# A 1 KB vector in a full DMA stream: one piece behind the start-up barriers, or sixteen pieces ahead of them

## The chip, the cores and the metric

The kernel runs on 1 core of one Trainium2 chip. The time is device microseconds of that core. A run of one core has no second die to compare with, so its state is called fast where it lies with the fastest runs of the same kernel; all runs here are fast but one, which is marked (a single run, state unknown). "The span" is the time from the first to the last instruction in the profile; it is 1.2 to 1.4 us shorter than the time of the same run.

## The reference

```python
B, S, D = 1024, 16, 512          # x, y: bf16 [1024, 16, 512]; gamma: bf16 [512]
def reference(x, y, gamma):
    return x + gamma * y
```

x and y are 16.78 MB each, and so is the result. Gamma is 1 KB.

## The kernel before

Each of the 128 partitions holds 128 rows of 512 elements. SP (SyncE) issues the loads of y and x, ACT (ScalarE) issues gamma and the two stores. `EARLY` says how many transfers of each of the two are put ahead of the program's start-up barriers, at which all engines wait for each other before the program proper begins (in the profile of before SP sits 0.2 us at the first of them and 0.5 us at the two that follow): one of SP (y's first half), none of ACT.

```python
SP = [('y', 0, 64), ('x', 0, 64, 0), ('y', 64, 128), ('x', 64, 117, 0), ('x', 117, 128, 64)]
ACT = [('g',), ('s', 0, 64), ('s', 64, 128)]
EARLY = (1, 0)
DVE = [('m', 0), ('m', 1), ('a', 0), ('a', 1), ('m', 2), ('m', 3), ('a', 2), ('a', 3)]
# ... (cut)
gamma_row = nc.alloc_sbuf_tensor("gamma_row", [1, D], dt).ap()
# ... (cut: in the loop that issues the transfers)
if kind == "g":
    i = eng.dma_start(out=gamma_row, in_=gamma.unsqueeze(0)).then_inc(s_gamma, 16)
# ... (cut)
# a row of ones times gamma's row: TensorE copies gamma to all 128 partitions
nc.tensor.matmul(gamma_ps, ones_row, gamma_row, start=True, stop=True).then_inc(s_ps, 1)
nc.vector.tensor_copy(out=gamma_sb, in_=gamma_ps).then_inc(s_dve, 1)
```

VectorE then multiplies y by gamma ("m") and adds x ("a"), in pieces of 53 and 11 rows. x's rows from 64 on go to the place of the first ones, so their load waits for the first add.

## Time and profile before

| | before |
|---|---|
| time, median of 6 runs | 120.09 us (119.85 to 120.28) |
| span in the profile | 118.6 us |
| the 16 DMA engines, two queues | 66.0% + 32.6% of the span |
| VectorE busy | 70.0 us, 59% |
| gamma: issue, landing, first use | 1.43, 9.60, 21.94 us |

The table of waits names who sat idle (engine, tile and line, what ended it: us in total, times, longest):

```profile
DVE y_sb L156 <- DVEq L25: 12.7, 2, 10.8
...
DVE y_sb L165 <- DVEq L25: 2.2, 1, 2.2
```

Line 156 is the multiply, line 165 the add, and line 25 is the helper that waits on a semaphore. VectorE waits 10.8 us for y ahead of the first multiply, and another 2.2 us for x ahead of the first add. The timeline (start, us, instruction) shows what that add releases:

```profile
41.39 17.29 DVE L165 TENSOR_TENSOR y_sb<-x_sb,y_sb 128x27136 bf16<-128x27136 bf16 x2 [2.16 <-DVEq L25]
55.71 0.81 SPq L113 DMA_DIRECT2D x_sb<-in_x_dram  x2
```

x's later loads are issued as soon as the first add is over; y's second half keeps the DMA engines busy until about 60 us (its last landing is at 60.49 us).

### The profile page before, as it was taken

The page shows a single profiled execution, that of the slowest core. Times are in us where ns is not written, and L with a number is a line of the kernel's source. Part 1 is how long each engine was busy: PE and PEld are TensorE (multiplying, and loading weights), DVE is VectorE, ACT ScalarE, POOL GpSimd, SP SyncE. Part 2 cuts the span into 40 slices and gives each one's busy share as a digit, 9 for nine tenths or more (in the row PEclk, how much of TensorE's full clock was granted, in tenths as well). Part 3 has the DMA queues.
Part 4 walks back from the last instruction along what each step waited for, and adds up shares of the span by engine and source line. Part 5 has one row for each costly group of instructions (what it writes and reads, how often), then busy time and mean ns, then how long its engine had stood idle before and what let it go on. Part 6 is the DMA issues. An engine that isn't in the chain of part 4 may idle for free. (4 is left out here: it accounts for less than half of the span.)

```text
span 118.6 us, 78 instructions
## 1 busy us (share of the span) xinstructions
PE 0.6 (0%) x1; PEld 0.1 (0%) x1; DVE 70.0 (59%) x10; POOL 0.2 (0%) x4
## 2 busy tenths in 40 slices
PE   0001000000000000000000000000000000000000
PEld 0000000000000000000000000000000000000000
DVE  0002000599999299999759999999999910000000
POOL 0000000000000000000000000000000000000000
DMA  9889888998899888998896969598899888988892
GB/s 354 354 376 685 354 354 354 597 464 354 354 398 663 354 354 354 663 398 354 354 586 293 586 293 567 220 639 354 354 575 486 354 354 376 685 354 354 354 619 88
DMA packets 1010, 50.33 MB, mean 424 GB/s; under 512 B 113, under 2 KB 114, under 8 KB 114
## 3 DMA queue, kind: packets, MB, share of 16 engines
q1 hardware_dynamic: 720, 33.55, 66.0%
q10 hardware_dynamic: 290, 16.78, 32.6%
HBM read 33.56 MB, written 16.78 MB: 424 GB/s over the span
## 5 line engine op out<-in xcount | busy, mean ns | idle before, releaser
L156 DVE TENSOR_TENSOR y_sb<-y_sb,gamma_sb 128x27136 bf16<-128x27136 bf16 (+1 forms) x4 | 34.6, 8688 | 12.7 <-DVEq L25 12.7
L165 DVE TENSOR_TENSOR y_sb<-x_sb,y_sb 128x27136 bf16<-128x27136 bf16 (+1 forms) x4 | 34.6, 8688 | 2.3 <-DVEq L25 2.2
L132 DVE CAST gamma_sb<-gamma_ps 128x512 bf16<-128x512 f32 x1 | 0.7, 692 | 8.8 <-DVEq L25 8.8
L127 DVE MEMSET ones_row<- 1x128 bf16 x1 | 0.2, 165 | 1.5 <-PEq L41 1.5
L130 PE MATMUL gamma_ps<-gamma_row,ones_row 1*128 1x512 bf16 x1 | 0.6, 578 | 9.7 <-PEq L25 9.7
L130 PEld LDWEIGHTS gamma_ps<-gamma_row,ones_row 1*128 1x128 bf16 x1 | 0.1, 100 | 9.7 <-issue 9.7
L194 POOL MEMSET const-uint8-127<- 128x1 uint8 x1 | 0.1, 102 | 0.0
L194 POOL MEMSET const-bfloat16-1.0<- 128x1 bf16 x1 | 0.1, 101 | 0.0
L194 POOL MEMSET const-float32-0.0<- 128x1 f32 x1 | 0.1, 98 | 0.2 <-issue 0.2
L194 POOL MEMSET const-float32-1.0<- 128x1 f32 x1 | 0.1, 98 | 0.0
## 6 DMA issues: line engine op xcount, KB each, us to landing
x_sb<-in_x_dram SPq DMA_DIRECT2D x1, 6784.0 KB, 20.8
x_sb<-in_x_dram SPq DMA_DIRECT2D x1, 1408.0 KB, 23.9
y_sb<-in_y_dram SPq DMA_DIRECT2D x2, 40.2
out_dram<-y_sb ACTq DMA_DIRECT2D x2, 22.8
x_sb<-in_x_dram SPq DMA_DIRECT2D x1, 39.7
gamma_row<-in_gamma_dram ACTq DMA_DIRECT2D x1, 1.0 KB
```

What stands on the lines that cost most here:

```text
L127: nc.vector.memset(ones_row, 1.0).then_inc(s_ones, 1)
L130: nc.tensor.matmul(gamma_ps, ones_row, gamma_row, start=True, stop=True).then_inc(s_ps, 1)
L132: nc.vector.tensor_copy(out=gamma_sb, in_=gamma_ps).then_inc(s_dve, 1)
L156: nc.vector.tensor_tensor(out=yt, in0=yt, in1=g, op=MULT).then_inc(s_dve, 1)
L165: nc.vector.tensor_tensor(out=yt, in0=xt, in1=yt, op=ADD).then_inc(s_add, 1)
L194: nc = _bacc.Bacc("TRN2", target_bir_lowering=False, num_devices=1)
```

## The change

Its intent: gamma is asked for at the very start and shared evenly among the engines, so that it arrives early and no one engine carries it alone. It becomes sixteen pieces of 64 B, meant as one for each DMA engine, which lie 128 B apart in one partition, and TensorE reads them as one row.

```diff
-EARLY = (1, 0)
+EARLY = (1, 1)
...
-    gamma_row = nc.alloc_sbuf_tensor("gamma_row", [1, D], dt).ap()
+    gamma_row = nc.alloc_sbuf_tensor("gamma_row", [1, 16, D // 8], dt).ap()[:, :, : D // 16]
...
-                i = eng.dma_start(out=gamma_row, in_=gamma.unsqueeze(0)).then_inc(s_gamma, 16)
+                src = gamma.rearrange("(a k d) -> a k d", a=1, k=16)
+                i = eng.dma_start(out=gamma_row, in_=src).then_inc(s_gamma, 16)
...
-    nc.tensor.matmul(gamma_ps, ones_row, gamma_row, start=True, stop=True).then_inc(s_ps, 1)
+    nc.tensor.matmul(gamma_ps.rearrange("p (k d) -> p k d", k=16), ones_row, gamma_row, start=True, stop=True).then_inc(s_ps, 1)
```

## The prediction

> **What bounds the kernel now.** I read the page first, from the busy times down to the DMA queues, to see which resource is full.
>
> ```profile
> PE 0.6 (0%) x1; PEld 0.1 (0%) x1; DVE 70.0 (59%) x10; POOL 0.2 (0%) x4
> ...
> DMA  9889888998899888998896969598899888988892
> ...
> DMA packets 1010, 50.33 MB, mean 424 GB/s; under 512 B 113, under 2 KB 114, under 8 KB 114
> ## 3 DMA queue, kind: packets, MB, share of 16 engines
> q1 hardware_dynamic: 720, 33.55, 66.0%
> q10 hardware_dynamic: 290, 16.78, 32.6%
> ```
>
> The two queue shares add up to 98.6% of sixteen engines over the whole span of 118.6 us. VectorE, the only compute engine with real work, is busy 59%. So the DMA engines are full, and bytes (x and y in, the sum out, 50.33 MB) set the time. The packet counts will matter too: seven large transfers (two of y, three of x, two stores) leave one 4 byte semaphore write per engine, 7 x 16 = 112, and 113 packets are under 512 B. The 113th is the single semaphore write of gamma, and the step from 113 to 114 is gamma itself, one packet of 1024 B.
>
> Then the timeline of the first 23 us and the table of waits, to see where gamma stands:
>
> ```profile
> 0.00 0.37 SPq L116 DMA_DIRECT2D y_sb<-in_y_dram  x1
> ...
> 1.43 0.33 SPq L113 DMA_DIRECT2D x_sb<-in_x_dram  x1
> 1.43 0.52 ACTq L110 DMA_DIRECT2D gamma_row<-in_gamma_dram  x1
> ...
> 9.73 0.58 PE L130 MATMUL gamma_ps<-gamma_row,ones_row 1*128 1x512 bf16 x1 [9.73 <-PEq L25]
> 10.46 0.69 DVE L132 CAST gamma_sb<-gamma_ps 128x512 bf16<-128x512 f32 x1 [8.78 <-DVEq L25]
> 21.94 14.29 DVE L156 TENSOR_TENSOR y_sb<-y_sb,gamma_sb 128x27136 bf16<-128x27136 bf16 x1 [10.79 <-DVEq L25]
> ```
>
> Gamma is asked for at 1.43 us, is spread over 128 partitions by 10.46 + 0.69 = 11.15 us, and is first used at 21.94 us. Between the two VectorE sits idle for 10.79 us. That wait ends with the first half of y, whose sixteenth landing the trace records at 21.81 us. So gamma has 10.8 us of slack, and the new date of its arrival can be worth nothing to VectorE.
>
> Last the chain that ended last, because the page names VectorE there:
>
> ```profile
> 77.99 0.08 issue
> 78.07 1.93 DVE y_sb L165
> 80.00 12.28 issue
> 92.28 3.08 DVE y_sb L165
> ```
>
> The last add ends at 95.36 us, and the second store is issued at 95.40 us; but the first store's packets run until 98.9 us, so the engines never stood empty for it. The chain is not the bound. I therefore went to the single packet records of the trace and strung each engine's packets together, each behind the one that had just ended. All sixteen strings run without a gap of over 15 ns, from a first packet at 1.00 to 1.63 us to an end between 117.65 and 118.23 us. The last store landing is at 118.57 us, the last instruction ends at 118.60 us, and the profiled run took 119.93 us, 1.33 us more than its span.
>
> The sum of one string: 50.33 MB / 16 = 3.146 MB = 48 packets of 65,536 B. One takes 2.418 us in the steady stretch, so 116.06 us. The slowest string starts at 1.33 us; its first packet took 2.89 us, 0.47 us more than a steady one; seven semaphore writes of 9 ns add 0.06 us. That is 1.33 + 116.06 + 0.47 + 0.06 = 117.92 us; the remaining 0.3 us are packets stretched where loads and the first store mix (76 to 79 us). So only three things can move the end: when y's first packets start, how long the first ones take, and what else is put on the slowest engine.
>
> [...]gamma's semaphore moves at 2.05 us, and then only at 9.60 us, when the one engine is done. [...]gamma's packet ran at 6.82 us for 46 ns between two 65,536 B packets, and its semaphore write at 9.28 us, after one more of them.[...]
>
> **The change part by part.** The order of instructions on every engine is the same but for one: ACT's gamma transfer moves ahead of the start-up barriers, as y's first load already stands on SP.
>
> 1. Removed: one 1024 B packet (46 ns) and one 4 byte write (9 ns) on one engine, 55 ns. In my strings that engine ended at 117.80 us, 0.43 us before the last. Worth to the end: 0. (With starts only some ns apart a string could be mistaken, so at most 0.055 us.)
> 2. Added: on each of 16 engines a 64 B packet and a 4 byte write. An instruction fetch of 40 B took 8 ns and the 1024 B packet 46 ns; a straight line between them gives 9 ns for 64 B. With the write 18 ns on every engine, hence also on the slowest: +0.02 us if they fall among y's packets, 0 if they run before them, when the engines are idle anyway.[...]
> 3. Moved on ACT: the issue (0.52 us before; 0.34 to 0.37 us for ACT's stores, which use 16 engines) now stands at about 0.1 us, ahead of ACT's first barrier step at 0.13 us. The first barrier, which released at about 0.65 us, will wait for it and slip by 0.1 to 0.3 us, and so will the two issues of SP that stood at 1.43 and 1.81 us. They queue behind a y load that lasts to 21.8 us: 0.
> 4. The start of y: the two issues now overlap. At 1.43 us SP's x and ACT's gamma already overlapped, and SP's took 0.33 us, as it did for x at 55.71 us with nothing beside it. So SP will not be held up. [...]y's 16 first packets, spread over 0.63 us, may come later by a share of that; I take +0.05 us as the middle, up to 0.3 us.
> 5. TensorE and VectorE: the matmul reads one row in 16 runs rather than in one; at 0.58 us, even a doubling is within the 10.8 us of slack. The cast, the multiplies and the adds stay as they are. 0.
>
> Sum: 0 + 0.02 + 0 + 0.05 + 0 = +0.07 us; from 120.16 us, 120.2 us.
>
> **The rivals.** (a) The balance pays: if the engine with gamma was the slowest, spreading gains up to 0.055 us, and early small packets may wake the path so that y's first packets lose their 0.3 to 1.0 us over the steady 2.42 us. Against: the string with gamma ended early, and the first packets of x and y later on were stretched by nothing such. It would give 119.9 us or less. (b) A wait takes the place of the one removed: gamma's pieces get in ahead of y, and y's first packets are held until those have landed. For: the start of y has no slack at all, every ns there is a ns at the end. Against: packets of one engine follow each other here without a gap, so a landing isn't waited for. It would give about 120.5 to 120.7 us. (c) The pieces reach the rings behind two y packets each and gamma lands at 7 to 10 us as before: hidden by the same slack, 120.2 us.
>
> **Range and chances.** The three runs before lie between 119.85 and 120.28 us, so 0.2 us either way is noise of the measurement; (a) pulls down by 0.2 us, (b) up by 0.4 us. I take 119.8 to 120.55 us. Two per cent is 2.4 us; no term above is a fifth of that but (b). Faster by 2% would need bytes to vanish; I give 0.005. Slower 0.01, within 2% 0.985.
>
> **What would show it.** The page should count 1010 - 2 + 32 = 1040 packets, 144 of them under 512 B and as many under 2 KB; the second queue 320. Gamma's issue should stand near 0.1 us; the matmul between 2 and 7.5 us rather than at 9.73; x's first issue at 1.5 to 1.8 us; the first multiply within 0.15 us of 21.94 us; the mean rate 423 to 425 GB/s. Step 4 is wrong if y's first packets start more than 0.15 us later, or sooner, than at 1.00 to 1.63 us. The prediction as a whole is wrong if gaps appear in an engine's string, or if the span moves by over 0.4 us with the first multiply at the same place.

The sum came to 0.02 us (part 2) and 0.05 us (part 4), +0.07 us together, so 120.2 us. The 0.05 us is my estimate, from the 0.63 us over which y's first packets spread. A dearer variant of part 2, +0.06 instead of +0.02 us, was not in the sum, and the ground for sixteen pieces on sixteen engines was assumed before the run and is seen in the records after it.

## The result, and the profile after

The changed kernel takes 120.13 us (median of 6 runs, 119.96 to 120.75) against 120.09 us before. The ratio is 1.001, with a 95% interval of 0.9986 to 1.0034: the same time. A ratio is the mean time of one kernel's fast runs over that of the other's of the same rounds, so it is not quite the ratio of the medians quoted. Again unaltered, in other rounds, it gave 0.9996 (0.9982 to 1.0011).

The page of the changed kernel, DMA rows and queues:

```profile
DMA  9889988998899888998896969698899889988891
...
DMA packets 1041, 50.33 MB, mean 424 GB/s; under 512 B 145, under 2 KB 145, under 8 KB 145
...
q1 hardware_dynamic: 720, 33.55, 66.0%
q10 hardware_dynamic: 320, 16.78, 32.6%
q14 instruction: 1, 0.00, 0.0%
```

The engines are as full as before, at the same 424 GB/s. Gamma's queue has 30 packets more: sixteen pieces and sixteen semaphore writes, for one of each before. The last line is a 40 B instruction fetch that fell just inside this span; the second profile of the same kernel doesn't have it and counts 1040.

The timeline of the changed kernel's first 23 us, and the add and the loads that it releases:

```profile
0.00 0.37 SPq L118 DMA_DIRECT2D y_sb<-in_y_dram  x1
0.13 0.58 ACTq L112 DMA_DIRECT2D gamma_row<-in_gamma_dram  x1
...
2.02 0.33 SPq L115 DMA_DIRECT2D x_sb<-in_x_dram  x1
...
9.99 0.58 PE L132 MATMUL gamma_ps<-gamma_row,ones_row 1*128 1x512 bf16 x1 [9.99 <-PEq L25]
...
22.06 14.29 DVE L158 TENSOR_TENSOR y_sb<-y_sb,gamma_sb 128x27136 bf16<-128x27136 bf16 x1 [10.65 <-DVEq L25]
...
41.52 17.29 DVE L167 TENSOR_TENSOR y_sb<-x_sb,y_sb 128x27136 bf16<-128x27136 bf16 x2 [2.16 <-DVEq L25]
55.84 0.81 SPq L115 DMA_DIRECT2D x_sb<-in_x_dram  x2
```

Three things are to be seen. Gamma's issue did move, from 1.43 to 0.13 us. Its arrival did not: the matmul starts at 9.99 us, later than the 9.73 us of before. And the barriers now end 0.6 us later (x's first issue, 1.43 to 2.02 us), with no effect on the first multiply, which still waits 10.65 us for y, nor on the first add.

The single packet records tell why gamma is no earlier. Its pieces run at 6.46 to 7.10 us, each behind the first two packets of y on its engine (the first start at 1.00 to 1.34 us, the second at 4.04 to 4.68 us). The semaphore writes follow one more packet of y later, and the last landing is at 9.86 us. Each piece takes 11 ns and each semaphore write 9 ns. The strings of the 16 engines end at 117.67 to 118.25 us, against 117.65 to 118.23 us before.

### The profile page after: what moved, and what is told of

The parts are those of the page before. It is cut to its first block, busy times and chain, and to the rows that moved or that the text cites. A ratio compares the mean times of both kernels' runs of the same rounds, so it can differ in the third digit from the quotient of the medians.

```text
span 118.7 us, 78 instructions
## 1 busy us (share of the span) xinstructions
PE 0.6 (0%) x1; PEld 0.1 (0%) x1; DVE 70.0 (59%) x10; POOL 0.2 (0%) x4
```

## The experiments

My theory: the 16 DMA engines each have a fixed share of a stream without a gap (none of over 15 ns in the strings of before), so the end moves only with the start of y and with what is put on the engine that ends last; gamma's date and its 20 to 55 ns of engine time are neither. The rivals are those of the prediction: that evenness pays, that small early packets help or hinder y's start, that the date of gamma counts. All twelve runs gave correct results. Runs of one call share the runs of the kernel before, given in brackets.

### One half of the change at a time

**The sixteen pieces, behind the barriers.**

```diff
-EARLY = (1, 1)
+EARLY = (1, 0)
```

> The sixteen pieces, but issued behind the barriers as before. Theory (nothing of gamma is on the path, the stream of the 16 DMA engines sets the end): 120.1 us, within 0.2 us of the kernel before; gamma's issue back at 1.43 us, x's first issue back at 1.43 us; the 64 B packets still run behind two packets of y each, at 6.4 to 7.2 us, the matmul at about 10 us. Rival (the pieces cost by themselves[...]): this run is as slow as the changed kernel and slower than the other half, by 0.1 us or more. Rival (being early matters to where gamma runs): the pieces run one packet of y later than in the changed kernel, at about 9 us.

Measured: 120.00 us (before 120.03); ratio 1.0001 (0.9985 to 1.0018). The pieces run at 6.41 to 7.16 us and the matmul at 10.07 us. Issued 1.3 us later than in the change, they run within 0.1 us of the same place. The pieces cost nothing that can be measured, and being early gained them nothing.

**One piece, ahead of the barriers.** This is the kernel before with only this line changed:

```diff
-EARLY = (1, 0)
+EARLY = (1, 1)
```

> Gamma as one piece of 1024 B, but issued early. Theory: 120.1 us, within 0.2 us of the kernel before; the one packet still runs behind two packets of y, at 6.4 to 7.0 us, its semaphore write 2.4 us later, the matmul at 9.3 to 10 us; the barriers slip by 0.5 to 0.6 us as in the changed kernel (x's first issue at about 2.0 us), for nothing. Rival (an early issue on ACT disturbs the start of y): y's second packets start later than in the kernel before by 0.1 us or more on the mean (before 4.32 us, changed 4.35 us), and the time rises by as much.

Measured: 120.13 us (before 120.03); ratio 1.0006 (0.9991 to 1.0022). The time is as expected, but two of the dates are not. The timeline:

```profile
1.73 0.33 SPq L113 DMA_DIRECT2D x_sb<-in_x_dram  x1
...
7.09 0.58 PE L130 MATMUL gamma_ps<-gamma_row,ones_row 1*128 1x512 bf16 x1 [7.09 <-PEq L25]
...
21.91 17.29 DVE L156 TENSOR_TENSOR y_sb<-y_sb,gamma_sb 128x27136 bf16<-128x27136 bf16 x2 [13.39 <-DVEq L25]
```

The single packet ran at 4.16 us, behind only one packet of y, and gamma landed at 6.96 us: 2.64 us sooner than before, where the sixteen early pieces gained nothing. The barriers slipped by 0.3 us, not by 0.5 to 0.6. VectorE merely waited longer for y, 13.39 us. So an arrival that really was 2.6 us earlier was worth nothing either. Why one early piece slips in ahead of y's second packet and sixteen don't is not settled here.

**The change again**, for a second profile:

> The changed kernel once more, unaltered, for a second profile and a tighter ratio. Theory: within 0.2 us of the kernel before; gamma's 64 B packets at 6.4 to 7.2 us again, the matmul at 9.9 to 10.1 us, the first barrier's slip of 0.6 us again; y's second packets at 4.25 to 4.36 us on the mean, so that the 0.04 us by which the first profile of the change was later than that of before lies within the scatter of one kernel. Rival (the change really delays y): 4.35 us or later again, and a time above that of the kernel before.

Measured: 119.96 us (before 120.05). The pieces start at 6.43 us, the matmul stands at 9.95 us. y's second packets start at 4.28 us on the mean, where the first profile of the change had 4.35 and the kernel before 4.32. The seven profiles that start as the change does, up to 2 us (the two of it, and five below that add to it later), give 4.26 to 4.44, on the mean 4.31 us; the four in which gamma is issued after the barriers give 4.27 to 4.32, on the mean 4.30 us. The change doesn't delay y by more than that scatter.

### What the start of y is worth

**Gamma ahead of y on SP, both early.**

```diff
-SP = [('y', 0, 64), ...      ACT = [('g',), ('s', 0, 64), ...      EARLY = (1, 1)
+SP = [('g',), ('y', 0, 64), ...      ACT = [('s', 0, 64), ...      EARLY = (2, 0)
```

> Gamma's sixteen pieces issued by SP, ahead of y's first load, both early. Theory (the start of y has no slack, gamma's date does not count): y's issue moves back by SP's issue time of about 0.4 us, its first packets start at 1.4 to 2.0 us, every later event shifts by the same, and the time rises by 0.3 to 0.5 us to about 120.5 us; gamma now runs before y's packets and lands by about 2.5 us, the matmul stands at about 2.7 us, and the first multiply still waits for y, at about 22.4 us. Rival (small packets first warm the path): y's first packets take near 2.42 us instead of 3.1 to 3.2 us, and the time is 119.9 us or less. Rival (y's first packets are held until gamma has landed): first packets at 2.5 us or later, 121 us or more.

Measured: 120.80 us (before 120.03); ratio 1.0064 (1.0049 to 1.0079), the upper side of what I had expected and more.

```profile
0.00 0.59 SPq L112 DMA_DIRECT2D gamma_row<-in_gamma_dram  x1
0.64 0.56 SPq L118 DMA_DIRECT2D y_sb<-in_y_dram  x1
...
2.80 0.58 PE L132 MATMUL gamma_ps<-gamma_row,ones_row 1*128 1x512 bf16 x1 [2.80 <-PEq L25]
```

In this timeline the issue of the pieces took 0.59 us, not 0.4, and y's own issue, right behind it, took 0.56 us instead of 0.37. y's first packets started 0.83 us later (1.83 us against 1.00), and the time rose by 0.77 us: what y's start loses, the end loses. Gamma landed at 1.79 us, 21 us before the first multiply. y's first packets still took 3.18 us on the mean (before 3.11 us), so nothing was warmed. That the first of them starts just after gamma's landing (1.83 against 1.79 us) looks like a wait for it, but the records speak against one: y's issue ended at 1.20 us, and its first packet started 0.63 us later. In all fourteen profiles, whatever gamma does, y's first packet starts 0.62 to 0.63 us after the end of y's issue.

**y's first load behind the barriers, gamma early**, so that gamma meets empty engines: `EARLY = (0, 1)`.

> Gamma early on ACT as in the change, but y's first load behind the barriers, so that gamma meets empty DMA engines. Theory: gamma lands about 2.0 us after its issue instead of 9.7 us, the matmul stands at 2 to 3 us; y is issued at about 1.7 to 2.0 us and the whole stream and the end shift by as much, to 121.8 to 122.2 us (span included, if it is counted from the first instruction). Rival (the start has slack, the end is set by VectorE or the last add): 120.1 to 120.5 us. Rival (gamma's landing is slow by itself, whatever the engines do): it lands at 9 us here too.

Measured: 122.05 us (before 120.03); ratio 1.0164 (1.0148 to 1.0181).

```profile
2.03 0.37 SPq L118 DMA_DIRECT2D y_sb<-in_y_dram  x1
...
2.58 0.58 PE L132 MATMUL gamma_ps<-gamma_row,ones_row 1*128 1x512 bf16 x1 [2.58 <-PEq L25]
```

y is issued at 2.03 us, its first packets start at 3.03 us, and the time is 2.02 us longer, nearly one for one. Gamma, alone, ran at 1.49 to 1.67 us (8 ns a piece) and landed by 1.93 us, 1.8 us after its issue. In the change its landing took 9.7 us from issue. The difference is the wait behind y: y's first packets are on the engines from 1.00 us, ahead of the 1.49 us at which the pieces could run.

### How late gamma may be

**Behind y's first load, on SP's queue**: `('g',)` moves to the second place in `SP`, `EARLY = (1, 0)`.

> Gamma's sixteen pieces on SP's own queue, behind y's first load: they can only run when y is through. Theory (gamma has slack beyond the first multiply too, since VectorE waits 2.2 us for x before the first add): the pieces run at 20.9 to 21.5 us, land at about 21.9 us, the first multiply starts 1.5 to 2 us later than before, at 23.5 to 24 us, the idle time ahead of the first add shrinks from 2.2 us to 0.2 to 0.7 us, and the time stays at 120.1 us (within 0.3 us). Rival (the date of gamma is on the path): the time rises by the 1.5 to 2 us of the multiply.

Measured: 120.02 us (before 120.10); ratio 1.0001 (0.9986 to 1.0016).

```profile
23.85 17.30 DVE L158 TENSOR_TENSOR y_sb<-y_sb,gamma_sb 128x27136 bf16<-128x27136 bf16 x2 [0.26 <-DVEq L25]
41.45 17.29 DVE L167 TENSOR_TENSOR y_sb<-x_sb,y_sb 128x27136 bf16<-128x27136 bf16 x2 [0.31 <-DVEq L25]
55.77 0.82 SPq L115 DMA_DIRECT2D x_sb<-in_x_dram  x2
```

Gamma landed at 22.04 us, 12 us later than in the change. The first multiply started 1.9 us later than before, and all of that came out of the wait for x (0.31 us left of 2.16). The first add, and the loads it releases, stand where they stood.

**Behind x's first load**: `('g',)` in the third place.

> Gamma still later, behind x's first load, to see that it can count at all. Theory: the first multiply starts at about 43 us, the two adds end at about 78 us, so x's second load is issued at 78 us, some 18 us after y's second load has left the engines at 60 us; a hole of 17 to 19 us in the DMA row, and the time rises by as much, to 137 to 140 us. Rival (a hole of that size is refilled because stores and loads can overlap later): under 130 us.

Measured, in one run only (state unknown): 136.99 us, just under the range I gave (before 120.10).

```profile
DMA  9997979879798797910000897996997987979876
...
43.24 17.29 DVE L158 TENSOR_TENSOR y_sb<-y_sb,gamma_sb 128x27136 bf16<-128x27136 bf16 x2 [0.26 <-DVEq L25]
60.69 17.29 DVE L167 TENSOR_TENSOR y_sb<-x_sb,y_sb 128x27136 bf16<-128x27136 bf16 x2
75.01 0.80 SPq L115 DMA_DIRECT2D x_sb<-in_x_dram  x2
```

The DMA row (40 slices of 3.4 us) has a hole from about 60 us until x's load, issued at 75.01 us, gets going. I had expected that issue at 78 us because I counted both adds; it needs the first one only (60.69 + 14.29 = 74.98 us). So gamma can count, once its lateness has used up every wait in front of the stream. The change is some 12 us away from that.

### What work on the engines costs

**127 more pieces of 64 B on every engine.** They sit behind y's first load on SP's queue and write to rows that y's second load overwrites, after a wait.

```diff
-SP = [('y', 0, 64), ('x', 0, 64, 0), ...
+SP = [('y', 0, 64), ('e',), ('x', 0, 64, 0), ...
...
+            elif kind == "e":
+                to = y_sb[:16, 64:, :].rearrange("p r (h d) -> p (r h) d", h=2)[:, :127, : D // 16]
+                src = gamma[: 16 * D // 16].rearrange("(k a d) -> k a d", k=16, a=1).to_broadcast([16, 127, D // 16])
+                i = eng.dma_start(out=to, in_=src).then_inc(s_extra, 16)
...
+                if w[1]:                 # y's second load
+                    _take(s_extra, 16, eng)
```

> The change, with 127 more pieces of 64 B on each of the 16 engines, behind y's first load on the same queue (copies of gamma into rows that y's second load overwrites later; the result stays right). Theory (each small packet takes 11 ns as in the changed kernel and each engine's stream is the bound): 127 x 11 ns + 9 ns = 1.4 us later at the end, 121.5 us.[...] Rival (small packets hide in gaps of the stream): within 0.3 us of 120.1 us.

Measured: 127.27 us (before 120.10); ratio 1.0591. This is no test of what I wanted. The timeline and the DMA row:

```profile
DMA  9799795189999999989998998889889989988970
...
2.40 19.44 SPq L120 DMA_DIRECT2D x_sb<-in_x_dram  x1
```

SP's issue of x took 19.44 us where it takes 0.33: it hung until y was nearly through. Then the engines stood mostly empty (the 5 and 1 in the row): between 22 and 26 us the records have 2.6 packets under way on the mean, of sixteen possible. The pieces themselves took 8 to 11 ns each in their records, but all 2,032 of them needed from 21.06 to 28.97 us, 3.9 ns a piece over the core, where sixteen engines with 11 ns each would need 0.7 ns a piece (1.4 us in all). What held them back is open: all read the same 1 KB and wrote to 16 partitions.

**The same 127 pieces on one engine**: in the lines of `to` and `src` every 16 but that of `D // 16` becomes 1.

> The same 127 pieces, all on one engine[...]. Theory (an engine's share is fixed and nobody takes work off it): that engine ends 127 x its packet time later, the others don't, and the end moves by this less the 0.1 to 0.5 us by which that engine was ahead of the last one: with 11 ns a packet +0.9 to +1.4 us, about 121.2 us, nearly as much as with all sixteen loaded. Rival (the engines share one rate, and the others gain what this one loses): a sixteenth of the other run's loss, under 0.2 us.

Measured: 121.72 us (before 120.10); ratio 1.0142 (1.0126 to 1.0159). The number is near my theory's, but for another reason: again SP's issue of x took long, 18.52 us, and x's packets began on all engines only at 21.93 us, instead of at 21 us. All strings ended 1.5 us later. (y's second load, which waits for the pieces, was issued at 22.45 us, 1.4 to 1.5 us after these 21 us; 127 pieces of 11 ns, one after the other, are 1.4 us by my estimate.) A pile of small pieces on one engine's queue stopped the issue for all sixteen. It doesn't tell the theories apart, so I made three runs with large packets.

**One packet of 64 KB more on one engine.** The lines of `to` and `src` become:

```diff
+                to = y_sb[:1, 64 : 64 + 64, :].rearrange("p r d -> p (r d)")
+                src = yv[:1, :64, :].rearrange("p r d -> p (r d)")
```

> The runs with 127 small pieces were no clean test: [...]all engines ran dry. This one puts a single packet of 64 KB more on one engine, behind y's first load (rows of y, into a place that y's second load overwrites later; the result stays right). Theory (an engine's share is fixed, the slowest engine sets the end): that engine ends 2.42 us later, less the 0 to 0.5 us by which it was ahead of the last: +2.0 to +2.4 us, 122.0 to 122.5 us, with no hole in the DMA row at 21 us. Rival (the engines share one rate): +0.15 us, 120.3 us.

Measured: 122.37 us (before 120.05); ratio 1.0203 (1.0181 to 1.0225), a loss of 2.3 us for 0.13% more bytes. The packet records show that engine end at 120.45 us while the other fifteen end by 118.95 us and take nothing off it. They also show a stretch at 79.5 to 80.0 us in which it alone is at work, and the others wait for the first store, which is held until x has landed on all engines. (The wait ahead of y's second load moves its issue from 2.40 to 24.04 us; in the next run it moves as well, to 22.20 us, at little cost, so that is not what the 2.3 us are.)

**16 KB more on one engine**: the same with 16 rows.

> 16 KB on one engine only, 0.60 us of its time: eleven times what gamma's one piece takes, and about as much as that engine was ahead of the last one (0.43 us in the profile of before). Theory: 0.1 to 0.6 us at the end, 120.2 to 120.7 us; a gamma of 0.055 us on one engine is then mostly lost in the lead of that engine, which is why spreading it gained nothing. Rival (each ns on any engine counts): +0.60 us. Rival (shared rate): +0.04 us, 120.1 us.

Measured: 120.24 us (before 120.05); ratio 1.0017 (1.0004 to 1.0031), so 0.05 to 0.37 us more for a packet of 0.611 us. The rest of it was lost in the lead of that engine: in the profile, its string ends at 118.36 us and another one last, at 118.48 us. Of the two rivals, "each ns counts" (0.60 us) is excluded, and the shared rate (0.04 us) is just outside the interval; the run with 64 KB excludes it by far.

**64 KB more on all sixteen engines**: as with one engine, with `:16` for `:1`.

> The same packet of 64 KB on each of the 16 engines. Theory: +2.42 us, 122.5 us, hardly more than with one engine loaded, though sixteen times the bytes are moved. Rival (one shared rate): also +2.4 us, so it is the pair of runs that tells. If the start-up or the receipts had slack, less than 2.2 us.

Measured: 130.09 us (before 120.05); ratio 1.0844. Neither theory had 10 us.

```profile
DMA  9897899009798798799798979799799799799792
```

The row has what looks like a hole (two slices of 3.2 us with 0), but the engines were not empty: the row books a packet in the slice in which it starts, and the records have sixteen packets under way all through it. They explain the loss in part: each of the sixteen extra packets took 8.0 to 9.5 us instead of 2.42. Together, 1.05 MB took from 20.91 to 31.17 us, 102 GB/s. They all went to partitions 0 to 15, unlike the large loads, which go to all 128; that this is the cause is my guess, for no run varied the partitions. As a partner to the run with one engine this one failed.

## Why the prediction was right

The time, 120.13 us against 120.2, and the verdict are right, and so is the reason for them: the stream of large packets sets the end, and gamma is not on its path. The sum of +0.07 us itself is below the 0.2 us of noise, so these runs neither confirm nor refute it. Not all steps were right.

1. *Removed, worth 0.* No run contradicts it, but the reading behind it was wrong. Where only one fits, a packet starts 3 or 4 ns before the one ahead of it on its engine ends; strung again by this rule, and so that each queue's packets keep their order on every engine, the records of before have the engine with gamma end at 118.01 or 118.23 us (the two can't be told apart), not at 117.80: at most 0.22 us ahead of the last, and perhaps the last itself. (So the slowest string, too, is another than the one in the prediction's sum.) In the run with one early piece it ended at about 117.9 us, some 0.35 us ahead of the last. A lead can swallow most of 0.6 us, as the 16 KB run shows; whether gamma's 55 ns fell into one is not shown. They are less than these runs resolve.
2. *Added, 18 ns on every engine.* Measured 11 + 9 = 20 ns. That is far from the dearer variant, a piece of 64 B as dear as one of 1024 B (46 ns).
3. *The barriers slip by 0.1 to 0.3 us.* The size was wrong: 0.59 us. I had expected an issue like that of ACT's stores, 0.34 to 0.37 us; the sixteen pieces took 0.58 us. And ACT's next instruction, the first barrier's drain, took 387 ns where it had taken 8. It cost nothing, as I had said, because x queues behind y.
4. *The start of y, +0.05 us.* SP's issue was not held up (0.37 us in both). The delay isn't there: y's second packets start at 4.31 against 4.30 us on the mean of the profiles. The 0.05 us should have been 0. One sign that I had named for this step being wrong did appear: the last of the sixteen first packets started 0.29 us sooner (1.34 us against 1.63). It told nothing: in the seven profiles that start as the change does, this packet starts anywhere between 1.34 and 2.15 us. That y's start is worth its full length at the end, on which the caution rested, is shown by the two runs that move it by 0.83 and 2.03 us and lose 0.77 and 2.02 us.
5. *TensorE and VectorE, 0.* Right: the matmul with sixteen runs takes 0.58 us as before, the first multiply stands at 22.06 us instead of 21.94.

Among the rivals, (a) found no gain anywhere, and (b) no wait. **The forecast that failed** is that of gamma's date: I said the matmul would move to between 2 and 7.5 us, and it went to 9.99. What I had kept as rival (c), that the pieces reach each engine behind two packets of y, is what happened. I had reckoned with gamma's issue and not with what is ahead of it on the engines. That gamma's packet of before had run between two packets of y (at 6.82 us, for 46 ns) did not tell it either: the pieces were issued by 0.71 us, y's second packets started only at 4.04 to 4.68 us, and still the pieces ran behind these. It did not matter because at 9.99 us the matmul is still far ahead of y: VectorE waits another 10.65 us. The slack is even longer than the 10.8 us that I named: the run with gamma 12 us later shows that the wait ahead of the add belongs to it as well.

No version here beats the kernel before; those that differ from it only in gamma's date, up to 22 us, have ratios to it between 0.9996 and 1.001, and no interval reaches beyond 1.0034.

## What to carry to other kernels

Where the DMA engines are full from end to end, ask of a small transfer only whether its reader waits for it and whether it delays the first large packets; being issued early does not by itself make it arrive early once large packets are ahead of it (sixteen early pieces gained nothing here, one gained 2.6 us). Put nothing ahead of the first large load (0.83 us of delay cost 0.77 us here), and don't load one engine with what costs a whole large packet, for nobody took it over here (64 KB on one engine cost 2.3 us, and the other fifteen ended 1.5 us or more before it). But 16 KB on one engine (0.61 us of its time) cost only some 0.2 us, and gamma's 55 ns can't be seen at all, so evening them out gained nothing that these runs could measure.

## What else the traces measured

- A load of 64 B took 11 ns among large packets (5.8 GB/s) and 8 ns on empty engines, against 2.418 us (27.1 GB/s) for a packet of 65,536 B. The piece took hardly longer than the 9 ns of a 4 B semaphore write, and far less than the 46 ns of 1024 B.
- With 127 pieces of 64 B queued on one engine, SP's next issue took 18.5 us instead of 0.33, and x's packets began on all engines only at 21.93 us instead of 21; with one packet of 16 or 64 KB in their place the issue took 0.34 to 0.35 us. How many pieces it takes, no run shows.
- 2,032 pieces of 64 B issued from SP took 7.9 us, 3.9 ns each over the core, though each is recorded with 8 to 11 ns on one of sixteen engines. The cause is open.
- ACT's drain behind its early issue of the sixteen pieces took 387 ns instead of 8, and with the issue itself the barriers ended 0.59 us later.
